# Loading the first two pairs' queries and keys four tokens to a partition, and transposing them on TensorE

## The chip, the cores and the metric

The kernel runs on one core of one Trainium2 chip. The metric is device time in microseconds (us) of one launch, the median of several runs. A profiled execution gives a trace beside it: the time of every instruction on TensorE (PE, with its weight loads as PEld), VectorE (DVE), ScalarE (ACT), GpSimd (POOL) and SyncE (SP), and of the transfers.

## The reference, cut to what matters

Attention with normalised queries and keys is followed by a gated feed-forward block.

```python
# q, k, v: (8, 12, 448, 64) float32; moe_w_*: float64, 768x1536, 768x1536, 1536x768
def rmsnorm(x, g):
    rms = np.sqrt(np.mean(x * x, axis=-1, keepdims=True) + 1e-06)
    return x / rms * g
q_n, k_n = (rmsnorm(q, g_q), rmsnorm(k, g_k))
scores = (1 / np.sqrt(64)) * np.matmul(q_n, k_n.transpose(0, 1, 3, 2))
attn = softmax(scores)                       # over the keys
x = np.matmul(attn, v) -> (8 * 448, 12 * 64) # token rows, heads side by side
g = x @ w_gate
out = (g / (1 + exp(-g)) * (x @ w_val)) @ w_out
```

## The kernel before, in words

The work is cut into 48 pairs: a pair is one batch and two heads, whose 2 x 64 head dimensions fill the 128 partitions. Two batches make a block of the feed-forward part; there are four blocks. The first 12 pairs ("early") come before any feed-forward work. The up products of a block (L1328, weights gate and value) and its down products (L1502) then fill TensorE, and the later pairs are worked in between the down products. The weights come as 64-bit floats. They are cast and summed into 15 combinations each (`convert`, L1120), written to DRAM (L1227) and read back as product weights (L1288). Six of the 24 weight pieces are converted among the early pairs, the others during the first block; those go into places that the early pairs use, after the last early pair has read them.

A pair is made by `attention` (L703). Its steps are these.

- `load` (L723): queries and keys, four loads each, one for each quarter of the partitions. A quarter holds one head and one half of the head dimension, so a row that is moved is 32 floats (128 bytes). All are issued by SP, but pair 0's keys by ACT.
- `square` (L754) on ACT, `summed` (L768) on DVE over each row of 32. Since a token's 64 values lie in two quarters, `swap` (L778, four ACT copies) exchanges the half sums and `both` (L782, DVE) adds them.
- `inverse_root` (L672): a logarithm and an exponential on ACT (L678, L679), three DVE steps (L684 to L686).
- `scale` (L795): two POOL multiplications, keys first.
- `transpose` (L811): two DVE transposes of 32x32 blocks. The queries go back into the buffer they were loaded in, and `queries` (L814, ACT) multiplies them by the gains' product `gg` (L1607) into the tile QT. The keys go to KT.
- `scores` (L840, PE), `exps` (L855, ACT), in four steps: keys 0 to 383 in three, the last 64 keys in a half step. Then `weighted` (L916, PE, values), `total` (L947, PE, sums of the exponentials), a reciprocal (L982, DVE), its spreading (L990, PE) and copy, addition and multiplication (L1005 ACT, L1008 and L1012 DVE). Sums of the finished pairs (L1049, L1053) feed the up products.

The loaded tiles have four buffers, so two pairs' queries and keys (`qk=4`, L547): the third pair's load waits until the first one's last reader is done. The tiles `t`, QT, KT, the two-bank score tile `st` and the output tile `at` have two each.

The order of the work is written by a planner, `Order` (L361). Every step is a piece with an engine, an assumed cost, a due time, the pieces it waits for and the buffers it takes. The planner runs a clock of its own through all the pieces and appends the instructions to each engine in the order that it finds. So a cost or a due time changes no instruction, only the order on each engine; on the chip each engine works through its queue in order. Early pairs are due from `LEAD`, one every `PAIR`, and everything later counts from these:

```python
LEAD, PAIR = 14.0, 9.0
FIRST = LEAD + EARLY * PAIR + 6.0
```

Of the kernel before, what the change touches and what calls it, by code (L numbers as in the profile page):

```python
# [477 lines left out]
def fast(  # L478
# [41 lines left out]
    nc = tc.nc  # L520
    B, H, S, D = q.shape
    DM = H * D
    DFF = moe_w_gate.shape[1]
    P = 128
    NJ = 4
# [5 lines left out]
    TB = 512  # L531
    NB = B // 2
    C = 32
# [2 lines left out]


    EARLY = 2 * NPAIR

    const = ctx.enter_context(tc.tile_pool(name="const", bufs=1))  # L540
    sbuf = ctx.enter_context(tc.tile_pool(name="sbuf", bufs=1))
# [5 lines left out]
        qk=4, v=2, t=2, QT=2, KT=2, e=4, ea=7, eh=2, sums=1, inv=1, rd=1, rows=3, st=2, at=2, ss=2,  # L547
        rr=4, ws=2, **{x + str(i): 1 for x in "vw" for i in range(6)},
# [6 lines left out]
    tiles = {}  # L555
# [10 lines left out]
    def take(name, key, shape):  # L566
        if name in ("e", "ea"):
            at = order.turn[name] % BUFS[name]
            tiles[name, key] = es[:, at] if at < BUFS["e"] else more_es[:, at - BUFS["e"]]
            return tiles[name, key]  # L570
        if name in OFTEN:
            at = OFTEN[name] + order.turn[name] % BUFS[name]
            tiles[name, key] = spare[:, ts(at, S)]
            return tiles[name, key]
        if name == "eh":
            at = order.turn["eh"] % BUFS["eh"]
            tiles[name, key] = more[:, at].rearrange("p (h q) -> p h q", h=2)
            return tiles[name, key]
        if name in WORK:
            at, size = WORK[name]  # L580
            at += order.turn[name] % BUFS[name] * size
            n = 1
            for length in shape[1:]:
                n *= length
            x = work[0 : shape[0], at : at + n]
            letters = "abcd"[: len(shape) - 1]
            x = x.rearrange(
                f"p ({' '.join(letters)}) -> p {' '.join(letters)}",
                **dict(zip(letters, shape[1:])),
            )  # L590
# [35 lines left out]
    many = const.tile([P, C], F32, name="many")  # L626
    halves = const.tile([P, 2, C], F32, name="halves")
    chosen = const.tile([P, 2, P], F32, name="chosen")
    gq2 = const.tile([P, 1], F32, name="gq2")
    gk2 = const.tile([P, 1], F32, name="gk2")  # L630
    gg = const.tile([P, 1], F32, name="gg")
# [1 line left out]

    LEAD, PAIR = 14.0, 9.0
    FIRST = LEAD + EARLY * PAIR + 6.0
    PRODUCT = 1.504
    UP, DOWN, BOTH = 30 * NG * PRODUCT, 90.7, 170.0
# [32 lines left out]
    def inverse_root(m, sums, of, when, rank=0.0):  # L672


        def estimate():
            ss = of()
            rr = take("rr", m, list(ss.shape))
            nc.scalar.activation(rr, ss, AF.Ln, scale=GAIN**-2)  # L678
# [24 lines left out]
    def attention(m):  # L703
# [14 lines left out]
        def add(*what, **more):  # L718
            return order.add(*what, rank=rank, **more)
# [2 lines left out]

        def load(x, src):  # L723
            def emit():
                to = take("qk", (m, x), [P, NC, C])
                for g in range(P // C):
                    rows = src[b, 2 * c + g // 2][:, ts(g % 2, C)]
                    queue.dma_start(to[ts(g, C)], rows.rearrange("(c i) f -> i c f", i=C))  # L728


            both = m == 0 and src is k
            queue = nc.scalar if both else nc.sync
            return add(
                "ACT" if both else "SP", 1.4 if both else 2.4, ready - 28.0, emit, takes=[("qk", (m, x))], kb=224, early=25.0,
                after=[staged.get(PAIRS)],
            )

        loaded = [load(x, src) for x, src in enumerate((q, k))]

        def load_values():  # L740
# [9 lines left out]

        def square(x):
            if x == 0:
                take("t", m, [P, 2, NC, C])
            nc.scalar.activation(tiles["t", m][:, x], tiles["qk", (m, x)], AF.Square)  # L754

        squares = []
        for x in range(2):
# [7 lines left out]


        def summed():
            nc.vector.tensor_reduce(  # L768
                out=take("ss", m, [P, 2, 2 * NC])[:, 0],
                in_=tiles["t", m].rearrange("p x c f -> p (x c) f"),  # L770
                axis=AX.X,
                op=ALU.add,
            )
# [12 lines left out]
        sums = add(  # L786
            "DVE", 1.1, ready - 17.0, summed, after=squares, uses=[("t", m)], takes=[("ss", m)]
        )
        sums = add("ACT", 0.9, ready - 16.0, swap, after=[sums], uses=[("ss", m)])
        sums = add("DVE", 0.15, ready - 15.0, both, after=[sums], uses=[("ss", m)])  # L790
        rr = inverse_root(m, sums, lambda: tiles["ss", m][:, 0], ready - 14.0, rank)

        def scale(x):
            rr = tiles["rr", m][:, ts(x, NC)].rearrange("p (c one) -> p c one", one=1)
            nc.gpsimd.tensor_tensor(  # L795
                out=tiles["t", m][:, x], in0=tiles["qk", (m, x)], in1=rr.to_broadcast([P, NC, C]),
                op=ALU.mult,
            )
# [7 lines left out]
        ]  # L806


        def transpose(x):
            to = take("KT", m, [P, S]) if x else tiles["qk", (m, 0)].rearrange("p c i -> p (c i)")  # L810
            nc.vector.transpose(to, tiles["t", m][:, x].rearrange("p c f -> p (c f)"))  # L811

        def queries():
# [2 lines left out]
                scale=gg,  # L816
            )

        kt = add(
            "DVE", 0.62, ready - 6.0, lambda: transpose(1), after=scaled[:1], takes=[("KT", m)],  # L820
            uses=[("t", m)],
        )
        qt = add(
            "DVE", 0.62, ready - 6.0, lambda: transpose(0), after=scaled[1:],
            uses=[("t", m), ("qk", (m, 0))],
        )
        qt = add(
            "ACT", 0.65, ready - 5.0, queries, after=[qt, gains], uses=[("qk", (m, 0))],
            takes=[("QT", m)],
        )  # L830
# [766 lines left out]
    for t, x in ((gq2, g_q), (gk2, g_k)):  # L1597
        col = x.rearrange("(d one) -> d one", one=1)
        nc.gpsimd.dma_start(t[0:64, :], col)
        nc.gpsimd.dma_start(t[64:128, :], col)  # L1600
    nc.vector.memset(chosen, 0.0)
    for i in range(P // C):
        h, half = divmod(i, 2)
# [94 lines left out]
```

## Time and profile before

| | |
|---|---|
| median of 3 runs | 1487.12 us |
| the runs | 1483.69 to 1489.3 us |
| profiled execution, first to last instruction | 1484.0 us (no further time of its own is given) |
| first product on PE | 14.66 us |
| first up product | 140.13 us |
| PE busy | 1425.0 us, 96% |
| DVE busy | 916.0 us, 62% |
| ACT busy | 681.5 us, 46% |
| POOL busy | 414.1 us, 28% |
| SP's first load of values issued | 7.50 us |

How to read it: a line of a timeline gives the start, the busy time, the engine, the line of the code, the operation with output and inputs, and in brackets how long the engine was idle before and who released it. "SPq" and "ACTq" are the queues where transfers are issued; the data lands later. A group of instructions has its busy time and the mean in ns of one. A product of 32-bit floats appears as two records. A line of stages gives, for each engine, its busy time and in brackets its instructions.

### The profile page before, as it was taken

The page shows a single profiled execution, that of the slowest core. Times are in us where ns is not written, and L with a number is a line of the kernel's source. Part 1 is how long each engine was busy: PE and PEld are TensorE (multiplying, and loading weights), DVE is VectorE, ACT ScalarE, POOL GpSimd, SP SyncE. Part 2 cuts the span into 40 slices and gives each one's busy share as a digit, 9 for nine tenths or more (in the row PEclk, how much of TensorE's full clock was granted, in tenths as well). Part 3 has the DMA queues.
Part 4 walks back from the last instruction along what each step waited for, and adds up shares of the span by engine and source line. Part 5 has one row for each costly group of instructions (what it writes and reads, how often), then busy time and mean ns, then how long its engine had stood idle before and what let it go on. Part 6 is the DMA issues. An engine that isn't in the chain of part 4 may idle for free.

```text
span 1484.0 us, 19470 instructions
## 1 busy us (share of the span) xinstructions
PE 1425.0 (96%) x6672; PEld 675.4 (46%) x6672; DVE 916.0 (62%) x1405; ACT 681.5 (46%) x1366; POOL 414.1 (28%) x468
## 2 busy tenths in 40 slices
PE   5789999999999999999999999999999999999998
PEld 2334544443444455544444445554444445555553
DVE  4777887877978544355886733454786854432533
ACT  6774544437775322445767422354676532122100
POOL 2454586636444100012544200011343410000000
PEclk9999999999999999999999999999999999999999
DMA  7767999974453432533344432352353442222235
GB/s 165 158 144 236 292 308 341 296 219 90 99 115 85 113 106 71 138 103 90 74 111 110 100 117 73 106 136 77 96 119 85 90 119 89 80 98 73 83 98 107
DMA packets 415921, 193.30 MB, mean 130 GB/s; under 512 B 324164, under 2 KB 397892, under 8 KB 409668
## 3 DMA queue, kind: packets, MB, share of 16 engines
q1 hardware_dynamic: 402688, 190.35, 48.0%
q10 hardware_dynamic: 12996, 1.61, 0.7%
q8 instruction: 55, 0.90, 0.3%
q14 instruction: 54, 0.44, 0.1%
q0 software_dynamic: 128, 0.00, 0.0%
HBM read 157.29 MB, written 34.60 MB: 129 GB/s over the span
## 4 chain that ended last, share of the span: by engine, by line
PE 73%; DVE 3%; ACT 2%; issue 1%; DMA 1%; SPq 1%; ACTq 0%; DVEq 0%
PE mm L1502 22%; PE mm L1328 20%; PE at L1328 20%; PE st L840 6%; PE at L916 5%; PE st L947 1%; ACT spare L1000 1%; ACT es L855 1%; DVE rd L982 1%; DMA out_dram<-spare 0%; SPq L728 0%; DVE ss L782 0%; DMA work<-in_k_dram 0%; DVE ss L768 0%; DVE sums L866 0%
## 5 line engine op out<-in xcount | busy, mean ns | idle before, releaser
L1328 PE MATMUL mm<-xs,ws 128*128 128x448 f32 x960 | 401.2, 540 | 4.4 <-DVE spare L1276 2.2
L1328 PE MATMUL at<-xs,ws 128*128 128x448 f32 x960 | 400.6, 540 | 4.1 <-DVE v L1274 2.6
L1328 PEld LDWEIGHTS mm<-xs,ws 128*128 128x128 f32 x960 | 181.5, 190 | 185.8 <-issue 173.8
L1328 PEld LDWEIGHTS at<-xs,ws 128*128 128x128 f32 x960 | 181.9, 190 | 184.6 <-issue 172.6
L795 POOL TENSOR_TENSOR work<-work,rr 128x448 f32<-128x448 f32 x96 | 105.9, 1122 | 503.5 <-DVE rr L686 245.2
L840 PE MATMUL st<-work 64*64 64x448 f32 (+1 forms) x1536 | 155.1, 508 | 27.3 <-ACT work L814 21.2
L1502 PE MATMUL mm<-gt,ws 128*128 128x448 f32 x448 | 177.2, 545 | 0.0
L1272 DVE TENSOR_TENSOR gt<-gt,mm 128x448 f32<-128x448 f32 x64 | 39.7, 621 | 185.1 <-PE mm L1328 171.3
L1502 PE MATMUL mm<-hs,ws 128*128 128x448 f32 x384 | 152.1, 545 | 0.9 <-DVE ss L684 0.9
L855 ACT ACTIVATE es<-st 128x896 f32<-128x896 f32 x129 | 114.3, 913 | 56.1 <-PE at L916 42.8
L860 POOL TENSOR_TENSOR sums<-es 128x896 f32<-128x896 f32 x36 | 75.7, 2104 | 195.8 <-PE st L947 83.2
L1402 ACT ACTIVATE st<-gt 128x448 f32<-128x448 f32 x96 | 52.4, 547 | 163.8 <-DVE gt L1276 85.9
L1000 ACT COPY spare<-rd 32x224 f32<-32x224 f32 x288 | 108.1, 375 | 35.0 <-DVE rd L982 30.7
L1502 PEld LDWEIGHTS mm<-gt,ws 128*128 128x128 f32 x448 | 82.9, 190 | 84.2 <-issue 81.0
L916 PE MATMUL at<-es,v 64*64 64x448 f32 x1032 | 110.2, 545 | 7.2 <-ACT xs L1005 3.3
L1270 ACT COPY gt<-mm 128x448 f32<-128x448 f32 x80 | 42.5, 531 | 141.5 <-PE mm L1328 141.4
L1502 PEld LDWEIGHTS mm<-hs,ws 128*128 128x128 f32 x384 | 71.1, 190 | 72.9 <-issue 70.9
L840 PEld LDWEIGHTS st<-work 64*64 64x64 f32 x1536 | 50.9, 134 | 108.7 <-issue 38.1
L1270 ACT COPY v<-at 128x448 f32<-128x448 f32 x96 | 51.1, 532 | 83.2 <-PE at L1328 80.0
L860 POOL TENSOR_TENSOR sums<-sums,es 128x896 f32<-128x896 f32 x36 | 78.7, 2187 | 2.8
L811 DVE STREAM_TRANSPOSE work<-work 128x448 f32<-128x448 f32 x96 | 59.2, 627 | 25.2 <-POOL work L795 23.1
L916 PEld LDWEIGHTS at<-es,v 64*64 64x64 f32 x1032 | 39.7, 134 | 67.4 <-issue 57.4
(150 smaller groups left out, 1568.7 us busy)
## 6 DMA issues: line engine op xcount, KB each, us to landing
ws<-up_sides SPq DMA_DIRECT2D x32, 1024.0 KB, 4.9
ws<-down_sides SPq DMA_DIRECT2D x16, 1024.0 KB, 5.0
ws<-down_sides SPq DMA_DIRECT2D x28, 512.0 KB, 4.0
ws<-up_sides SPq DMA_DIRECT2D x16, 768.0 KB, 4.6
work<-in_q_dram SPq DMA_DIRECT2D x192, 56.0 KB, 2.4
work<-in_k_dram SPq DMA_DIRECT2D x188, 56.0 KB, 2.5
out_dram<-spare SPq DMA_DIRECT2D x168, 56.0 KB, 1.9
v<-in_v_dram SPq DMA_DIRECT2D x96, 96.0 KB, 2.5
```

The lines of the kernel that those rows point to most:

```text
L795: nc.gpsimd.tensor_tensor(out=tiles["t", m][:, x], in0=tiles["qk", (m, x)], in1=rr.to_broadcast([P, NC, C]), op=ALU.mult,)
L811: nc.vector.transpose(to, tiles["t", m][:, x].rearrange("p c f -> p (c f)"))
L840: nc.tensor.matmul(st[ds(D * x, D), h, 0:n], tiles["KT", m][rows, ds(P * j + D * of_keys, D)], tiles["QT", m][rows, ds(Q * of_queries, n)] ...
L855: nc.scalar.activation(e, tiles["st", (m, j)][:, :, 0 : S * width(j) // P], AF.Exp)
L860: nc.gpsimd.tensor_tensor(out=to, in0=tiles["e", (m, 0)] if j == 1 else to, in1=e, op=ALU.add)
L916: nc.tensor.matmul(tiles["at", (m, x)][ds(D * h, D), queries], tiles["v", m][rows, j, h], tiles["e", (m, j)][rows, h], start=j == 0, stop= ...
L1000: nc.scalar.copy(inv[ds(D * h + C * to, C), ts(x, Q)], tiles["rd", m][ds(D * h + C * x, C)])
L1270: nc.scalar.copy(to, ps)
L1272: nc.vector.tensor_tensor(out=to, in0=old, in1=ps, op=ALU.add)
L1328: nc.tensor.matmul(ps(), w[:, at, which, c], xs[:, SLOT[x], c], start=fresh and c == 0, stop=c == NC2 - 1, skip_group_check=True,)
L1402: nc.scalar.activation(take(*act, [P, 2, TB])[:, 0, 0:S], to, AF.Silu)
L1502: nc.tensor.matmul(banks[s][:, 0:S], w[:, at, s, g], where[x][:, g], start=fresh and g == 0, stop=g == NG - 1, skip_group_check=True,)
```

## The change

For pairs 0 and 1 (`NATURAL`), a partition holds four consecutive tokens: 112 partitions (`R = S // NJ`), two heads, 4 x 64 values of each, so a row that is moved is 1 KB and queries or keys are one load. A token's 64 values lie in one partition. The square and the sum run on 112 partitions and rows of 512; the sum is over 64, and a small DVE addition takes the place of `swap` and `both`. `scale` writes the products in the order token quarter, head, dimension. Then TensorE transposes each quarter (112 tokens by 128) against an identity into a score tile in PSUM, keys first (`turn`). A copy out of PSUM restores the order of the tokens (`drain`): keys on DVE, queries on ACT with the gain. The identity is made on POOL at the start, before its first multiplication. After pair 0's second square, TensorE is given four products of 512 columns on pair 0's keys, whose results nobody reads. `LEAD` becomes 10.0, so all due times of early pairs and of what follows are 4 earlier. The other 46 pairs are worked as before.

In the built program, the order of the instructions differs on every engine within the early pairs; after PE's first up products nearly all of it is the same. ACT's order at the start is now: squares of pair 0 and of pair 1's queries, pair 0's root, the square of pair 1's keys, pair 1's root, pair 0's queries, its two first exponentials, pair 1's queries, a weight cast, pair 2's squares, pair 0's second large exponential, pair 2's swap and root, pair 3's squares, pair 0's third. PE's is: four dummy products, 8 transposes, half step and first step of pair 0's scores, 8 transposes, then more scores. SP's register load of the flag `fits` (L1665) stands among pair 4's loads, where it stood behind the first product weights.

```diff
+    NATURAL = (0, 1)
+    R = S // NJ
+    ident = const.tile([P, P], F32, name="ident")
-    LEAD, PAIR = 14.0, 9.0
+    LEAD, PAIR = 10.0, 9.0
...
         def load(x, src):
             def emit():
+                if natural:
+                    to = take("qk", (m, x), [R, 2, NJ * D])
+                    rows = src[b][2 * c : 2 * c + 2].rearrange("h (p j) d -> p h (j d)", j=NJ)
+                    queue.dma_start(to, rows)
+                    return
...
+            nc.scalar.activation(tiles["t", m][:, x], of, AF.Square)
+            if m == 0 and x:
+                for _ in range(4):
+                    nc.tensor.matmul(banks[0], chosen[0:R, 0], of, start=True, stop=True)
...
         def summed():
+            if natural:
+                ss = take("ss", m, [P, 2, 2 * NC])
+                sums = ss[0:R, 0, 0 : 4 * NJ]
+                nc.vector.tensor_reduce(
+                    out=sums, in_=tiles["t", m].rearrange("p x (n d) -> p (x n) d", d=D), axis=AX.X,
+                    op=ALU.add,
+                )
+                nc.vector.tensor_scalar_add(sums, sums, D * 1e-6)
+                return
...
-        sums = add("ACT", 0.9, ready - 16.0, swap, after=[sums], uses=[("ss", m)])
-        sums = add("DVE", 0.15, ready - 15.0, both, after=[sums], uses=[("ss", m)])
+        if not natural:
+            sums = add("ACT", 0.9, ready - 16.0, swap, after=[sums], uses=[("ss", m)])
+            sums = add("DVE", 0.15, ready - 15.0, both, after=[sums], uses=[("ss", m)])
...
         def scale(x):
+            if natural:
+                split = dict(h=2, j=NJ, d=D)
+                rr = tiles["rr", m][:, ts(x, 2 * NJ)].rearrange("p (h j one) -> p h j one", h=2, one=1)
+                nc.gpsimd.tensor_tensor(
+                    out=tiles["t", m][:, x].rearrange("p (j h d) -> p h j d", **split),
+                    in0=tiles["qk", (m, x)].rearrange("p h (j d) -> p h j d", d=D),
+                    in1=rr.to_broadcast([R, 2, NJ, D]), op=ALU.mult,
+                )
+                return
...
+        def turn(x):
+            if x:
+                take("st", (m, "turned"), [P, 2, TB])
+            turned = tiles["st", (m, "turned")][:, x]
+            for j in range(NJ):
+                nc.tensor.transpose(turned[:, ts(j, R)], tiles["t", m][:, x, ts(j, P)], ident[0:R, 0:R])
+
+        def drain(x):
+            turned = tiles["st", (m, "turned")][:, x, 0:S].rearrange("p (j r) -> p r j", j=NJ)
+            to = take("KT" if x else "QT", m, [P, S]).rearrange("p (r j) -> p r j", j=NJ)
+            if x:
+                nc.vector.tensor_copy(out=to, in_=turned)
+            else:
+                nc.scalar.activation(to, turned, AF.Copy, scale=gg)
...
+    make_identity(nc, ident)
     nc.vector.memset(chosen, 0.0)
```

More of the change, by code (lines that the diff above doesn't have):

```diff
@@ L676, in estimate @@
             ss = of()
-            rr = take("rr", m, list(ss.shape))
+            rr = take("rr", m, [P, 2 * NC])[0 : ss.shape[0], 0 : ss.shape[1]]
+            tiles["rr", m] = rr
             nc.scalar.activation(rr, ss, AF.Ln, scale=GAIN**-2)
@@ L733, in load @@
             return add(
-                "ACT" if both else "SP", 1.4 if both else 2.4, ready - 28.0, emit, takes=[("qk", (m, x))], kb=224, early=25.0,
+                "ACT" if both else "SP", 0.5 if natural else 1.4 if both else 2.4, ready - 28.0, emit, takes=[("qk", (m, x))], kb=224, early=25.0,
                 after=[staged.get(PAIRS)],
             )
+        natural = m in NATURAL
         loaded = [load(x, src) for x, src in enumerate((q, k))]
@@ L752, in square @@
             if x == 0:
-                take("t", m, [P, 2, NC, C])
-            nc.scalar.activation(tiles["t", m][:, x], tiles["qk", (m, x)], AF.Square)
+                take("t", m, [R, 2, 2 * NJ * D] if natural else [P, 2, NC, C])
+            of = tiles["qk", (m, x)]
+            if natural:
+                of = of.rearrange("p h f -> p (h f)")
+            nc.scalar.activation(tiles["t", m][:, x], of, AF.Square)
+            if m == 0 and x:
+                for _ in range(4):
+                    nc.tensor.matmul(banks[0], chosen[0:R, 0], of, start=True, stop=True)
         squares = []
@@ L788, in attention, with sums_of @@
         )
-        sums = add("ACT", 0.9, ready - 16.0, swap, after=[sums], uses=[("ss", m)])
-        sums = add("DVE", 0.15, ready - 15.0, both, after=[sums], uses=[("ss", m)])
-        rr = inverse_root(m, sums, lambda: tiles["ss", m][:, 0], ready - 14.0, rank)
-        def scale(x):
+        if not natural:
+            sums = add("ACT", 0.9, ready - 16.0, swap, after=[sums], uses=[("ss", m)])
+            sums = add("DVE", 0.15, ready - 15.0, both, after=[sums], uses=[("ss", m)])
+        def sums_of():
+            return tiles["ss", m][0:R, 0, 0 : 4 * NJ] if natural else tiles["ss", m][:, 0]
+        rr = inverse_root(m, sums, sums_of, ready - 14.0, rank)
+        def scale(x):
+            if natural:
+                split = dict(h=2, j=NJ, d=D)
[6 more added lines that the diff above has]
+                return
             rr = tiles["rr", m][:, ts(x, NC)].rearrange("p (c one) -> p c one", one=1)
@@ L817, in queries @@
             )
-        kt = add(
+        kt = qt = None
+        if natural:
+            of_turned = ("st", (m, "turned"))
+            kt, qt = [
+                add(
+                    "PE", 0.8, ready - 6.0, lambda x=x: turn(x), after=[scaled[1 - x]],
+                    uses=[("t", m)] + [of_turned] * (1 - x), takes=[of_turned] * x, mode="full",
+                )
+                for x in (1, 0)
+            ]
+            kt = add(
+                "DVE", 0.64, ready - 5.0, lambda: drain(1), after=[kt], takes=[("KT", m)],
+                uses=[of_turned],
+            )
+            qt = add(
+                "ACT", 0.6, ready - 5.0, lambda: drain(0), after=[qt, gains], takes=[("QT", m)],
+                uses=[of_turned],
+            )
+        kt = kt or add(
             "DVE", 0.62, ready - 6.0, lambda: transpose(1), after=scaled[:1], takes=[("KT", m)],
@@ L822, in attention @@
         )
-        qt = add(
+        qt = qt if natural else add(
             "DVE", 0.62, ready - 6.0, lambda: transpose(0), after=scaled[1:],
@@ L826, in attention @@
         )
-        qt = add(
+        qt = qt if natural else add(
             "ACT", 0.65, ready - 5.0, queries, after=[qt, gains], uses=[("qk", (m, 0))],
```

## The prediction, made before the run

> **What bounds the kernel now.** I read the page's chain of waits and then the busy time by stage, to learn which stage can still give time.
>
> ```profile
> PE 73%; DVE 3%; ACT 2%; issue 1%; DMA 1%; SPq 1%; ACTq 0%; DVEq 0%
> ```
>
> The chain that ended last is TensorE (PE) work for three quarters of the span. The stages, with columns PE, weight load, DVE, ACT, POOL, clock, DMA share, GB/s:
>
> ```profile
> 0.00:20.00 20.00, 5.34 (x40) 1.98 (x40) 7.47 (x23) 9.18 (x22) 6.56 (x16) 1.00 0.76 146
> 20.00:140.00 120.00, 100.21 (x1164) 44.84 (x1157) 92.71 (x151) 83.61 (x160) 59.96 (x91) 0.99 0.71 172
> 140.00:330.00 190.00, 183.62 (x487) 91.61 (x486) 154.01 (x231) 83.19 (x113) 112.42 (x218) 1.00 0.95 293
> ```
>
> PE idles 14.7 us in the first stage, 19.8 in the twelve early pairs (20 to 140), 6.4 in the first block's up products, and hardly after. So what starts the pairs earlier can move the whole run, if the pairs pass it on. The timeline of the start shows the chain to the first product:
>
> ```profile
> 5.85 0.58 ACT L754 ACTIVATE work<-work 128x448 f32<-128x448 f32 x1 [2.96 <-DMA work<-in_k_dram]
> 7.15 0.58 ACT L754 ACTIVATE work<-work 128x448 f32<-128x448 f32 x1 [0.73 <-DMA work<-in_k_dram]
> ...
> 7.76 1.09 DVE L768 TENSOR_REDUCE ss<-work 128x28 f32<-128x896 f32 x1 [4.38 <-ACT work L754]
> ...
> 8.88 0.88 ACT L778 COPY ss<-ss 32x28 f32<-32x28 f32 x4 [1.15 <-DVE ss L768]
> ...
> 10.02 0.23 ACT L678 ACTIVATE rr<-ss 128x28 f32<-128x28 f32 x1 [0.25 <-DVE ss L782]
> ...
> 11.39 1.83 POOL L795 TENSOR_TENSOR work<-work,rr 128x448 f32<-128x448 f32 x2 [7.79 <-DMA v<-in_v_dram]
> ...
> 13.94 0.67 ACT L814 ACTIVATE work<-work,gg 128x448 f32<-128x448 f32 x1 [0.44 <-DVE work L811]
> ...
> 14.66 5.02 PE L840 MATMUL st<-work 64*64 64x224 f32 x32 [14.66 <-ACT work L814]
> ...
> 15.19 2.54 SPq L728 DMA_DIRECT2D work<-in_q_dram  x4
> ...
> 21.25 1.88 SPq L728 DMA_DIRECT2D work<-in_q_dram  x4
> ...
> 23.94 1.04 ACT L754 ACTIVATE work<-work 128x448 f32<-128x448 f32 x2
> ```
>
> The load, square, sum, half swap, root, scale, transpose and gain follow each other with nothing beside them, to 14.66. The two SPq lines show a second effect: pair 2's q load leaves just after pair 0's L814 ended (14.61), pair 3's just after pair 1's ended (20.57 + 0.66), since they take the buffers that L814 reads. Third, the first scores, by shape:
>
> ```profile
> L840 PE MATMUL st<-work 64*64 64x448 f32 x24 | 4.2, 864 | 0.0
> L840 PE MATMUL st<-work 64*64 64x224 f32 x8 | 1.0, 604 | 14.7 <-ACT work L814 14.7
> L916 PE MATMUL at<-es,v 64*64 64x448 f32 x8 | 0.9, 536 | 0.0
> ```
>
> The same width takes 864 ns among the first and 536 soon after: a slow start, though the page's granted clock reads 9 there.
>
> [...] No trace here shows a TensorE transpose. [...] the old loads are rows of 128 B, and 0 to 10 us moves 112 GB/s at a DMA share of 0.76, where 140 to 150 us moves 315 at 0.99. [...]
>
> **The change, part by part.**
>
> *Loads.* Sixteen loads (four of them on ACT) become four: rows of 1 KB. K of pair 0 still leaves ACT at 1.63. Loads at that line took 1.8 to 5.7 us to land, median 3.1; 224 KB in one piece beside three more I put at 3.4, so 5.0 instead of 7.15: -2.1 (bounds -3.7 and 0). SP reaches the values' loads at 2.3 instead of 7.50, -5.2.
>
> *Norm of pair 0.* Rows are 512 wide on 112 partitions: square 0.58 x 512/448 = 0.66 (+0.08), reduce 1.09 x 1024/896 = 1.25 (+0.16). The swap and its add go: 8.85 to 10.02 was 1.17, a small add takes about 0.3: -0.85. Roots stay (10.02 to 11.17). From there to the first score it was 3.49. Now: two scales 2 x 0.93 x 512/448 = 2.14 with 0.2 ahead, four transposes 0.8 (224 columns take 0.38 at L990, two passes; so 112 take 0.19), drain 0.67, hops 0.25: 4.06, +0.57. The gain gg now stands on DVE behind pair 1's root steps and pair 0's key drain: +0.4 (0 to 0.8). Sum: -2.1 + 0.08 + 0.16 - 0.85 + 0.57 + 0.4 = -1.7. Scores start at about 12.9.
>
> *Dummy products.* Four of 512 columns, two passes each. A 448-column pass takes 1.504/4 = 0.376 at L1328, so 0.43 here, 0.86 at half clock. [...] The query transposes can't start before 10.7, so they cost nothing; all slow they end at 11.9 and cost 1.2. If they work, the first 16 records take the 1.36 us that the later group (26.47) takes. The first large exp started 17.24 - 14.66 = 2.6 after the scores; now 1.4: -1.2. It starts at 14.3, -2.9 in all.
>
> *Identity.* A memset and a select of 128x128 on POOL at 3.6; not in the trace. The nearest row, a 128x128 add at L1202, takes 0.45 to 0.5 us. Between 0 and 3 us it is covered by POOL's wait to 11.39 (now about 8.4); beyond 4 it delays every scale. I take 0.
>
> *Buffers.* Natural pairs free their q buffer after the scale, about 10.7 and 14.0, not after L814. With SP ahead, pair 2's k lands near 18.5 (squares were at 23.94) and pair 3's near 23 (28.65): -5.4.
>
> *Queue order.* ACT's queue now has pair 0's second and third large exps behind a weight cast and the squares of pairs 2 and 3, and PE has pair 1's transposes ahead of pair 0's later scores. Walked with the rows' durations: second exp 19.0 (was 18.73), third ends 24.5 (was 20.62), pair 1's last ends 29.8 (was 30.46). So pair 0 gets later, pair 1 equals, and pairs 2 and 3 are prepared 5 us sooner. SP's register load moves from 128.2 to about 20: 0.75 + 0.19 plus gaps, up to 1.4 us ahead of pair 4's loads. SP has slack there, I take 0.
>
> *What passes on.* DVE is 77% busy from 20 to 140. Before 30 us it did 2.56 + 4.91 + 4.37 = 11.8 us of work. In the new order it can do the memsets (1.2) and checks (0.6), norm and drains of pairs 0 and 1 (2 x 2.8), norm and transposes of pairs 2 and 3 (2 x 2.9), the first join (0.6) and part of a reciprocal (1.0): 14.8, 3.0 ahead. The exps give 2.9, the loads 5.4; I take 3.2 for the end of the pairs. After that, nearly all queues stand in the old order. The next weights take the places that the last early pair leaves, so they move too: of PE's 6.4 idle us in that stage most wait for DVE, 0.87 for weights. I take full carry; the bounds are 0 and 3.2. The profiled execution has a span of 1484.0 and shows nothing around it; its own sum is 1480.8. The runs' median is 1487.12, 3.1 above, so: 1487.1 - 3.2 = 1483.9.
>
> **Rivals.**
>
> *Swallowed* (0.20): the pairs are held by DVE and by loads landing late (ACT stood 2.56 us for pair 5's keys at 54.98), or the first block waits longer for weights, its DMA share being 0.95. For it: pair 1's exps gain only 0.7. Against: DVE idled 6.7 us at 25 and 3.86 at 55. Result 1487.1.
>
> *Cold anyway* (0.12): the dummies end, PE idles[...]; or they end late. The 1.2 is lost, and up to 1.2 more hides the transposes: 3.2 - 1.7 = 1.5, so 1485.6.
>
> *All of it* (0.12): DVE fills its early holes and the loads' 5.4 comes through, with the reorder worth another 1: 1487.1 - 6.4 = 1480.7.
>
> *Slower by ACT's queue* (0.11): pair 0's third exp stands behind the squares of pair 3. If that pair's keys land behind a 1152 KB weight block (at 264 GB/s 4.4 us), at 27.5, pair 1's exps end at 34.3 and not 30.46: +3.9. The same order again at pairs 4 and 5 gives as much: +7.9, 1495.0. It decides from a landing at about 23.7. Against: DMA share was only 0.55 from 20 to 30.
>
> **How the numbers follow.** Forecast 0.45 at 1483.9. Half a per cent, 7.4 us, is about what a measurement of this kernel tells from no change; the three runs lie 5.6 apart. Faster by that needs under 1479.7: the most favourable part of "all of it" and of the forecast, 0.10. Slower needs over 1494.6: 0.10. The rest, 0.80, is within. The range of 1479.0 to 1490.5 holds the forecast, cold and swallowed cases with 3 us of spread and half of "all of it"; it leaves out the slower one.
>
> **What would show it.** First score near 12.9 and the first large exp near 14.3; 448-column scores near 540 ns from the start; dummies over by 10.5; pair 2's squares near 18.5 and pair 3's near 23; first up product at 137 and not 140.13; last first-block product 3 us before 328.4. It is wrong if ACT waits for pair 3's keys past 25, if a POOL select runs past 8 us, or if the first up product comes early and the block's weight waits grow by as much.

## The result, and the profile after

After the change the median is 1483.66 us (20 runs, 1481.1 to 1485.94), before it is 1487.33 (20 runs, 1483.69 to 1489.3). The ratio is 0.9977, 95% interval 0.9971 to 0.9983: about 3.4 us less. The profiled execution after spans 1482.6 us and its run took 1484.42. That difference of 1.8 lies around every profiled execution below, so the profiled one of before (1484.0) was a run of about 1485.8, 1.5 under its median, and that of after lies 0.8 over its own. Two single traces therefore differ by only 1.4 us, and no conclusion here rests on the two spans.

The chain of waits of the kernel after looks as before: TensorE for three quarters.

```profile
PE 73%; ACT 3%; DVE 3%; issue 1%; DMA 1%; SPq 1%; ACTq 0%; DVEq 0%
```

The stages of the kernel after, columns as in the prediction (PE, weight load, DVE, ACT, POOL, clock, DMA share, GB/s):

```profile
0.00:20.00 20.00, 11.06 (x39) 5.33 (x40) 6.59 (x20) 6.54 (x12) 7.46 (x18) 0.91 0.72 161
20.00:140.00 120.00, 105.47 (x1185) 46.74 (x1184) 91.39 (x152) 85.08 (x161) 54.46 (x81) 0.94 0.68 169
140.00:330.00 190.00, 184.28 (x490) 92.23 (x489) 156.59 (x234) 84.79 (x118) 118.93 (x228) 1.00 0.95 293
```

PE is busier in the first two stages (11.06 and 105.47, were 5.34 and 100.21), but 6.75 us of it are dummies, and in the second stage part of the busy time is products at half clock (0.94, was 0.99). So busy time alone shows no gain. The start has to be read step by step; the timeline of the kernel after:

```profile
1.61 0.41 ACTq L732 DMA_DIRECT2D work<-in_k_dram  x1
3.92 0.29 POOL masks.py:199 TENSOR_SCALAR_AFFINE_SELECT ident<-ident 128x128 f32<-128x128 f32 x1
6.71 1.15 ACT L767 ACTIVATE work<-work 112x512 f32<-112x512 f32 x2 [2.29 <-DMA work<-in_k_dram]
6.83 6.75 PE L770 MATMUL mm<-work,chosen 112*128 112x512 f32 x8 [6.83 <-DMA work<-in_k_dram]
7.38 1.22 DVE L787 TENSOR_REDUCE ss<-work 112x16 f32<-112x1024 f32 x1 [2.65 <-ACT work L767]
8.84 0.22 ACT L682 ACTIVATE rr<-ss 112x16 f32<-112x16 f32 x1 [0.97 <-DVE ss L791]
10.07 2.04 POOL L827 TENSOR_TENSOR work<-work,rr 112x512 f32<-112x512 f32 x2 [5.85 <-DVE rr L690]
13.41 0.93 PE L853 MATMUL st<-ident,work 112*128 112x112 f32 x8
14.38 0.62 DVE L859 COPY work<-st 128x448 f32<-128x448 f32 x1 [2.24 <-PE st L853]
15.51 0.16 DVE L1680 SCALAR_TENSOR_TENSOR gg<-gq,gk 128x1 f32<-128x1 f32 x1
15.77 0.63 ACT L861 ACTIVATE work<-st,gg 128x448 f32<-128x448 f32 x1 [3.13 <-DVE gg L1680]
16.45 1.02 PE L912 MATMUL st<-work 64*64 64x224 f32 x8 [2.11 <-ACT work L861]
```

The first score starts at 16.45, which is 1.8 later than before (14.66), though the run is faster. Four things are to be seen. The keys' landing lets the square start at 6.71. The dummies end at 13.58, and the key transposes wait for that: their scale was done near 11.1. The copies out of PSUM follow each other, and the second waits for `gg`, which DVE makes at 15.51 behind pair 1's root steps.

The first products of the kernel after by shape (mean ns is the number after the busy time):

```profile
L770 PE MATMUL mm<-work,chosen 112*128 112x512 f32 x8 | 6.7, 1025 | 6.8 <-DMA work<-in_k_dram 6.8
L912 PE MATMUL st<-work 64*64 64x224 f32 x8 | 1.0, 605 | 2.1 <-ACT work L861 2.1
```

The scores of 224 columns take 605 ns, as long as the 604 of before: the dummies did not make them faster. The next view, four short stretches of the kernel after (columns of the stages), shows why:

```profile
6.30:9.60 3.30, 2.77 (x4) 1.25 (x5) 1.63 (x4) 1.88 (x5) 0.00 (x0) 1.00 0.63 101
9.70:13.00 3.30, 3.30 (x6) 1.24 (x5) 2.37 (x4) 0.55 (x3) 2.04 (x2) 1.00 0.95 294
13.10:16.40 3.30, 1.24 (x10) 0.74 (x8) 1.21 (x5) 0.63 (x1) 0.76 (x1) 1.00 0.86 157
16.50:19.80 3.30, 3.30 (x21) 1.65 (x22) 0.00 (x0) 1.31 (x2) 1.18 (x2) 0.50 0.38 63
```

The clock column is the one ahead of the last two. It says 1.00 in the first two rows too, where the passes took 1025 ns (in e7 the median pass took 592): this trace's first record of the clock is at 13.03, and ahead of it the column says nothing. From 13.1 the 1.00 is real (eight transposes in 0.93 us), and it is 0.50 from 16.5, when the scores begin. Behind the dummies the clock was at 1.00, and by the time of the first score it was at 0.50.

### The profile page after: what moved, and what is told of

Same layout as the page of the kernel before. It is cut to its first block, busy times and chain, and to the rows that moved or that the text cites. A ratio compares the mean times of both kernels' runs of the same rounds, so it can differ in the third digit from the quotient of the medians.

```text
span 1482.6 us, 19482 instructions
## 1 busy us (share of the span) xinstructions
PE 1435.1 (97%) x6696; PEld 680.7 (46%) x6696; DVE 914.8 (62%) x1403; ACT 680.7 (46%) x1358; POOL 416.0 (28%) x470
## 4 chain that ended last, share of the span: by engine, by line
PE 73%; ACT 3%; DVE 3%; issue 1%; DMA 1%; SPq 1%; ACTq 0%; DVEq 0%
PE mm L1574 22%; PE mm L1400 20%; PE at L1400 20%; PE st L912 6%; PE at L988 5%; PE st L1019 1%; ACT spare L1072 1%; ACT es L927 1%; SPq L737 1%; DVE rd L1054 1%; DVE ss L807 0%; DMA work<-in_k_dram 0%; DMA out_dram<-spare 0%; DVE ss L793 0%; ACT ss L803 0%
## 5 line engine op out<-in xcount | busy, mean ns | idle before, releaser
L834 POOL TENSOR_TENSOR work<-work,rr 128x448 f32<-128x448 f32 x92 | 101.8, 1126 | 480.1 <-DVE rr L690 353.3
```

The source lines that it names most:

```text
L834: nc.gpsimd.tensor_tensor(out=tiles["t", m][:, x], in0=tiles["qk", (m, x)], in1=rr.to_broadcast([P, NC, C]), op=ALU.mult,)
```

## The experiments

The theory after the first reading: the start became no earlier, so the gain must come from the order of the instructions, which the prediction had put at nothing. The rival: it comes from the new data path (fewer loads, no swaps, SP free sooner). Two times of each trace are compared, the first score and the first up product, with the stage between them:

| kernel | first score, us | first up product, us | stage, us | median, us | ratio to before, 95% interval |
|---|---|---|---|---|---|
| before | 14.66 | 140.13 | 125.5 | 1487.33 | |
| after | 16.45 | 139.92 | 123.5 | 1483.66 | 0.9977, 0.9971 to 0.9983 |
| e4, before again | 14.60 | 139.06 | 124.5 | 1486.41 | 0.9999, 0.9990 to 1.0007 |
| e2, due times only | 14.54 | 140.97 | 126.4 | 1486.45 | 0.9999, 0.9990 to 1.0007 |
| e9, weights behind keys | 14.68 | 141.53 | 126.9 | 1487.59 | 1.0000, 0.9991 to 1.0008 |
| e6, new path, old order | 16.66 | 143.71 | 127.1 | 1486.20 | 0.9994, 0.9987 to 1.0000 |
| e5, old path, new order | 16.57 | 137.90 | 121.3 | 1483.14 | 0.9970, 0.9959 to 0.9981 |
| e11, as e5, gain first | 16.23 | 136.93 | 120.7 | 1484.14 | 0.9978, 0.9971 to 0.9985 |
| e1, no dummies | 16.22 | 136.62 | 120.4 | 1483.21 | 0.9976, 0.9966 to 0.9987 |
| e3, early dummies | 16.62 | 140.20 | 123.6 | 1484.30 | 0.9979, 0.9971 to 0.9988 |
| e7, twelve dummies | 23.30 | 144.99 | 121.7 | 1490.37 | 1.0018, 1.0008 to 1.0028 |
| e10, start mended | 13.08 | 136.33 | 123.3 | 1479.91 | 0.9955, 0.9942 to 0.9969 |
| e8, all early natural | 16.51 | 135.62 | 119.1 | 1492.60 | 1.0034, 1.0023 to 1.0046 |
| e12, preparation first | 16.34 | 147.1 | 130.8 | 1494.03 | 1.0047, 1.0032 to 1.0061 |

Each ratio is to runs of before that were made beside that kernel, so it is not the quotient of two medians of the table. The times of the first score, the first up product and the stage are those of one trace each.

### Taking the parts away: e1, e2, e3, e4

e1 is the kernel after without the dummies:

```diff
-            if m == 0 and x:
-                for _ in range(4):
-                    nc.tensor.matmul(banks[0], chosen[0:R, 0], of, start=True, stop=True)
```

> The changed kernel without its four dummy products; the order on every engine is otherwise the same. In the profile of the changed kernel the dummies ran at half clock from 6.83 to 13.58 and the key transposes started at 13.41, while the scaled keys were there at about 11.1. Theory A (the dummies are a cost where they stand): first score at about 15 and not 16.45, and the run is equal to the changed kernel or up to 1.5 us faster, 0.9967 to 0.9977 of before. Rival (the dummies pay by warming the array): the first scores become slower still, and the run loses 1 to 2 us, 0.9985 to 0.999 of before.

Measured: 0.9976 beside 0.9977 with them, as the theory had it; but the first score came at 16.22, not at about 15. Its start, PE and the chain ahead of it:

```profile
9.77 0.22 ACT L682 ACTIVATE rr<-ss 112x16 f32<-112x16 f32 x1 [0.97 <-DVE ss L788]
12.10 2.01 PE L850 MATMUL st<-ident,work 112*128 112x112 f32 x8 [12.10 <-POOL work L824]
15.53 0.64 ACT L858 ACTIVATE work<-st,gg 128x448 f32<-128x448 f32 x1 [1.96 <-DVE gg L1677]
16.22 2.52 PE L909 MATMUL st<-work 64*64 64x224 f32 x16 [2.11 <-ACT work L858]
```

In this trace pair 0's keys landed 0.9 later than in after (7.62 and 6.69), so the root began at 9.77 and not 8.84. From the root to the first score it is 6.45 us, with dummies 7.61: the dummies cost 1.2 us at this place. The eight transposes take 2.01 here and 0.93 behind the dummies. A difference of 1.2 at the start doesn't show in the medians (1483.21 and 1483.66, intervals overlap).

e2 is the kernel before with the new due times only; it tells the change of order that they bring alone from that which the new pieces bring. e4 is the kernel before, unchanged.

```diff
-    LEAD, PAIR = 14.0, 9.0
+    LEAD, PAIR = 10.0, 9.0
```

> The kernel before with LEAD 10 in place of 14 and nothing else: the order on PE and POOL stays word for word, 26 lines of DVE, 42 of ACT and 20 of SP change. Theory A (the gain comes from the pairs' new data path and the order that follows from it): within 1 us of before, 0.9993 to 1.0007. Rival (the gain is the shifted due times): as the changed kernel, 0.997 to 0.998.

> The kernel before, unchanged: a second trace, and what the comparison makes of no change. 1.000 within 0.0006. If stages vary from one execution to the next, the first up product (140.13 in the first profile) and the span (1484.0) move by 1 to 4 us and show in which stage; if the first profile is typical they stay within 0.5 us.

Both measured 0.9999, so the due times alone are worth nothing, and the comparison itself is good to about 0.1%. In e2, PE's and POOL's queues are those of before; 26 instructions of DVE, 42 of ACT and 20 of SP stand elsewhere. But all of these stand behind the first up product (on SP near 265 us, on DVE from about 610). Among the early pairs e2 runs in the order of before, so it says that the due times change nothing there without the new pieces; it is no test of the new order. In e4 the first up product came 1.1 us earlier than in the first trace of the same kernel, so a stage varies by that much at least.

e3 has eight dummies of 256 columns on a constant tile, without waiting for a load, in place of the four:

```diff
-            if m == 0 and x:
-                for _ in range(4):
-                    nc.tensor.matmul(banks[0], chosen[0:R, 0], of, start=True, stop=True)
...
+    for _ in range(8):
+        nc.tensor.matmul(
+            banks[0][:, 0 : 2 * P], chosen[:, 0], chosen.rearrange("p x f -> p (x f)"),
+            start=True, stop=True,
+        )
```

> The changed kernel with its dummy products replaced by eight of 256 columns on the constant tile, which need no load; they should run from about 2 to 9 us. Theory A (dummies late, in the way of the transposes): first score at 14 to 15, and if the array stays at full clock until then the first 448-column scores take near 540 ns and not 951; 1 to 2 us faster than the changed kernel, 0.9965 to 0.997. Rival (the start is not on the path that sets the end): the start moves and the run stays at 0.9977 within 0.0006.

Measured 0.9979, and the first score came at 16.62, not at 14 to 15. The dummies start at 1.86 and end at 7.15, PE then idles 5.34 us, and the transposes at 12.49 take 2.01 us again, as in e1, at a clock of 0.50: dummies that early brought the transposes nothing.

### Order or data path: e5, e6, e11

In these kernels the planner is replaced by a fixed list of pieces, so that one kernel's instructions are issued in the other's order:

```diff
-    def run(self, lookahead=400):
...
+    def run(self):
+        left, at = [], 0
+        for step in STEPS.split():
+            at += int(step)
+            left.append(self.pieces[at])
+        while left:
+            i = next(i for i, piece in enumerate(left) if self.start(piece) is not None)
+            piece = left.pop(i)
```

e5 has the loads and transposes of before in the order of after; apart from the replaced instructions its queues are those of after. e6 has the loads, transposes and dummies of after in the order of before.

> The kernel before (old loads, swap, DVE transposes, no dummies) with the pieces of work emitted in the changed kernel's order; swap stands behind the sum and the old transposes and gain stand where the new drains stand. Theory B (the gain is the new order of the early pairs' work on the engines, which the new pieces gave to the planner): 0.997 to 0.9985 of before. Rival theory C (the gain is the new data path: larger rows, earlier free buffers): 1.000 or slower, up to 1.003, since the order was made for shorter steps.

> The changed kernel's data path for pairs 0 and 1, dummies included, with the pieces of work emitted in the order of the kernel before. Theory B (order): 0.9995 to 1.001 of before, although pair 2's and 3's loads go earlier. Theory C (data path): 0.997 to 0.9985. If the two effects add, this ratio times that of the old path in the new order gives the 0.9977 of the changed kernel.

Measured: e5 0.9970, the whole gain without any of the new instructions; e6 0.9994, at most a small part of it with all of them. That settles order against path. Whether the two add isn't told: the product of the two ratios is 0.9964, against 0.9977 for after, and each is good to about 0.001. The stage from the first score to the first up product says it again: in the order of before it took 124.5 to 127.1 us (five traces, mean 126.0), in that of after 120.4 to 123.6 (after, e1, e3, e5, e7, e10, e11; mean 122.1). From the first up product to the end both orders take the same, 1344.3 and 1344.2 us. So the order is worth 3.9 us of this stage; one trace of an order can lie 3 us from another. The 3.9 is idle time of PE: between these two marks it idles 17.1 to 19.8 us in the five traces of the old order (mean 18.2) and 12.3 to 16.0 in the seven of the new (mean 14.3).

What it does, in stretches of the kernel before:

```profile
20.00:30.00 10.00, 8.01 (x100) 3.56 (x92) 4.37 (x8) 8.72 (x18) 0.47 (x1) 1.00 0.55 96
40.00:50.00 10.00, 7.90 (x100) 3.37 (x98) 8.27 (x17) 7.33 (x15) 3.34 (x5) 1.00 0.73 180
50.00:60.00 10.00, 6.38 (x85) 2.58 (x81) 5.67 (x11) 6.46 (x14) 3.96 (x9) 1.00 0.63 155
```

and of e5, which has the same instructions:

```profile
20.00:30.00 10.00, 3.63 (x32) 1.21 (x32) 4.19 (x9) 8.16 (x21) 1.84 (x2) 0.81 0.83 186
40.00:50.00 10.00, 9.30 (x112) 3.83 (x108) 9.23 (x17) 9.00 (x17) 4.34 (x7) 1.00 0.53 95
50.00:60.00 10.00, 10.00 (x120) 4.45 (x116) 8.30 (x15) 9.16 (x17) 7.78 (x14) 1.00 0.90 268
```

The new order loses at first: PE is busy 3.6 of 10 us instead of 8, since ACT prepares pairs 2 and 3 between pair 0's exponentials, and ACT's copy of pair 0's output starts at 35.59 (before 24.93). From 30 to 70 PE then idles 0.7 us in all, where that of before idles 8.5, of which 2.1 at 40 to 50 and 3.6 at 50 to 60. The other traces say the same: 6.2 to 9.6 us in the five of the old order, 0.4 to 3.8 in the seven of the new. By the same copy, pair 4 is ahead in the new order (72.44, was 73.55), pair 5 once more behind (82.24, was 80.68), and from pair 7 on each is 1.5 to 2.9 ahead, pair 11 at 135.49 (was 137.72).

e11 is e5 with `gg` made right behind pair 0's root, one step of the list moved:

```diff
-    '1 1 32 1 -32 1 1 31 -30 1 1 29 -28 1 28 359 -358 1 1 -30 31 -30 55 -54 30 -43 14 1 29 24 -52 29 -27 '
+    '1 1 32 1 -32 1 1 31 -30 1 1 29 -28 1 -10 38 359 -358 1 1 -30 31 -30 55 -54 30 -29 1 29 24 -52 29 -27 '
```

> The old data path in the new order (0.997 of before) with the gain moved right behind pair 0's root on DVE. First score at 14.6, as before, and not 16.57. If the start is passed on: 0.9955 to 0.996. Rival (lost again): 0.9965 to 0.9975.

Measured 0.9978, a little above the rival's range, its interval overlapping that of e5. The first score came at 16.23, not at the expected 14.6: in the old path the queries' gain doesn't wait for `gg`, because the DVE transposes come later still.

### Is a late start passed on: e7 and e10

e7 runs twelve dummies instead of four.

```diff
-                for _ in range(4):
+                for _ in range(12):
```

> The changed kernel with twelve dummy products in place of four, so that the first transposes and pair 0's scores come some 7 to 13 us later (half clock until about 13.6 us, 0.84 us a pass, then either clock). Theory: the start of the scores has slack, because pair 0's later exponentials wait in ACT's queue behind the squares of pairs 2 and 3 anyway; then the run loses less than half of the delay of the first score, 0.9977 to 1.000. Rival (the recorded view: the start is passed on): the run loses the whole delay, 1.002 to 1.006.

The first score came 6.85 us later than after's, the median 6.7 us (6.1 by the ratios). So the delay is passed on, and the theory of slack has fallen. PE then is fast: 16 scores of 224 columns in 1.36 us (after 2.52), the first large exponential 1.43 behind the first score (after 2.59), which doesn't pay for the delay.

e10 mends the start of the kernel after: no dummies, pair 0's keys on SP right behind its queries, and `gg` on DVE right behind pair 0's root (a step of the list); all else in after's order.

```diff
-            both = m == 0 and src is k
+            both = False
...
-            if m == 0 and x:
-                for _ in range(4):
-                    nc.tensor.matmul(banks[0], chosen[0:R, 0], of, start=True, stop=True)
```

> The changed kernel's data path and order without dummies, with two moves: pair 0's keys are loaded on SP right after its queries (they landed 5 us after issue, behind pair 1's), and the gain stands on DVE right behind pair 0's root. First score at 12 to 13.5 and not 16.2. If the start is passed on, as twelve dummies' 6.85 us was, the run is 3 to 4 us faster than the changed kernel: 0.9945 to 0.996. Rival (a gain at the start is lost to the waits for loads): 0.9965 to 0.998.

Measured 1479.91 (5 runs), 0.9955, the fastest of all: 3.75 us under after by the medians, 3.3 by the ratios, for a first score 3.4 earlier. Its start:

```profile
4.82 0.63 ACT L873 ACTIVATE work<-work 112x512 f32<-112x512 f32 x1 [0.21 <-DMA work<-in_k_dram]
7.38 0.20 ACT L788 ACTIVATE rr<-ss 112x16 f32<-112x16 f32 x1
9.68 2.01 PE L956 MATMUL st<-ident,work 112*128 112x112 f32 x8 [9.68 <-POOL work L930]
11.73 0.63 DVE L962 COPY work<-st 128x448 f32<-128x448 f32 x1 [1.07 <-PE st L956]
12.39 0.63 ACT L964 ACTIVATE work<-st,gg 128x448 f32<-128x448 f32 x1 [1.23 <-DVE work L962]
13.08 2.52 PE L1015 MATMUL st<-work 64*64 64x224 f32 x16 [1.38 <-ACT work L964]
```

The keys' square starts at 4.82 (6.71), and the queries' gain no longer waits for `gg` but for the key copy. Beside e1, which differs by the two moves alone, the root begins 2.4 us earlier (7.38, was 9.77) through the keys, and the first score 3.1 earlier; the rest is `gg`'s. The median is 3.3 us under that of e1, where the two intervals overlap a little. The traced run is the slowest of e10's five (1482.43), so that its stage of 123.3 is likely long. So the new path can give an earlier start, about what the prediction said, once pair 0's keys stand second among the loads and the gain isn't late. e7 and e10 both say that a microsecond at the start is nearly a microsecond at the end. Not tried: the loads and transposes of before in the new order with pair 0's keys second on SP. How much of e10's start belongs to the new path, and how much to the place of the keys, is therefore open.

### Where in the order: e9, e12, e8

e9 is the kernel before with one thing moved: SP's fourth load of a weight piece stands behind pair 5's queries and keys. In before, ACT waited 2.56 us for those keys. The order of SP's queue, the only one that differs (the register load of `fits` comes forward too, to about where after has it):

```diff
+TensorLoad fits
+DMACopy work<-in_q_dram 32x14x32 x4
+DMACopy work<-in_k_dram 32x14x32 x4
 DMACopy gt<-in_moe_w_val_dram 128x2x128 x2
 DMACopy gt<-in_moe_w_val_dram 128x3x128
 DMACopy gt<-in_moe_w_val_dram 128x128 x2
-DMACopy work<-in_q_dram 32x14x32 x4
-DMACopy work<-in_k_dram 32x14x32 x4
...
-TensorLoad fits
```

> The kernel before with one thing changed: on SP the load of the fourth weight piece stands behind pair 5's queries and keys, as in the changed kernel's order, and not ahead of them (SP's register load moves too). All other engines keep the old order. Theory D (the new order gains because pair 5's keys no longer land behind a weight piece: before, ACT waited for them 2.56 us and DVE stood 3.86 us at 55): pair 5's squares at about 50 and not 54.98, and 0.997 to 0.9985 of before. Rival (the gain is the order of the work on ACT, DVE and PE, more pairs prepared ahead of the exponentials): 0.9993 to 1.0007.

Measured 1.0000. Two stretches of e9:

```profile
50.00:60.00 10.00, 8.78 (x112) 3.71 (x105) 8.36 (x17) 8.89 (x17) 7.29 (x13) 1.00 0.89 252
60.00:70.00 10.00, 6.63 (x52) 2.36 (x56) 6.12 (x7) 6.06 (x9) 4.60 (x7) 0.91 0.65 126
```

The hole at 50 to 60 is filled (PE 8.78, was 6.38), and the next stretch has it instead (6.63, was 9.28), with ACT waiting 3.87 us for the next queries. In this trace the hole is moved, not closed. But its place isn't fixed: in e4, the unchanged kernel, ACT waited only 0.48 us for pair 5's keys and PE was busy 8.96 us at 50 to 60, with the hole at 40 to 50 (7.23). So the wait of 2.56 belongs to that one execution, and it is the ratio that says the theory has fallen.

e12 is the kernel before with only the preparation of pairs in the order of after (a list again); PE's queue is that of before to the instruction. DVE's order around pair 0's reciprocal, for one:

```diff
 TensorReduce ss<-work 128x28
-TensorTensor xs<-xs,at 128x448
-Reciprocal rd<-mm 128x224
 TensorScalarPtr ss<-ss 128x28
...
 TensorReduce ss<-work 128x28
+TensorTensor xs<-xs,at 128x448
+Reciprocal rd<-mm 128x224
 StreamTranspose work<-work 128x448 x2
```

> The kernel before, with its own loads, transposes and instructions; only the pieces that prepare a pair (loads of queries and keys, squares, sums, swaps, roots, scales, DVE transposes, gains) stand at the places that they have in the order of the kernel after, and all else, scores and exponentials and weights too, keeps the order of before. TensorE's queue is then that of before, instruction for instruction. Theory one, the order of after gains because the preparation of the pairs runs further ahead of the exponentials: ratio 0.997 to 0.9985, and from the first score to the first up product about 122 to 123.5 us. Theory two, the gain needs TensorE's and the exponentials' order too (pair 1's first products ahead of pair 0's later ones): ratio 0.9993 to 1.0010, and 125 to 127 us for that stage. The first score is expected at 14.6 to 16.6 us in both.

Measured 1.0047: neither theory's number, and the theory that preparation ahead is the gain by itself has fallen. DVE and PE of e12 around 30:

```profile
29.11 1.09 DVE L873 TENSOR_REDUCE ss<-work 128x28 f32<-128x896 f32 x1 [1.80 <-ACT work L859]
30.64 1.55 DVE L1087 RECIPROCAL rd<-mm 128x224 f32<-128x224 f32 x1
32.24 1.23 PE L1095 MATMUL mm<-rd,chosen 128*128 128x224 f32 x4 [4.15 <-DVE rd L1087]
```

Pair 0's reciprocal stands on DVE behind pair 3's sum, and that behind the square of keys that landed near 28.5. It starts at 30.64 (before 26.61), and PE, whose old order has the spreading product ahead of pair 1's work, stands still for 4.15 us. This is kin to the prediction's slower rival: the cause is the same, keys of pair 3 that land late, but what waits for them is DVE's reciprocal and not ACT's exponential. That the price comes near the rival's 1495.0 is in part chance. The first score of e12 is 1.7 later too, and after the wait PE is at half clock for some 6.8 us (the mean of 30 to 40 is 0.66); over 20 to 140 the mean clock is 0.91 (before 0.99). In the kernel after, PE has pair 1's products at that place.

e8 brings all twelve early pairs in the new way, and the planner orders them:

```diff
-    NATURAL = (0, 1)
+    NATURAL = tuple(range(2 * NPAIR))
```

> The changed kernel with all twelve early pairs loaded four tokens to a partition and transposed on TensorE. Theory C (the data path helps every pair it is used for: rows of 1 KB, no swap, 0.9 us of ACT less a pair): 0.993 to 0.9965. Theory B (it is the order): anything between 0.995 and 1.004, the planner making another order. Against it: 16 transposes and a score tile more for each pair on TensorE.

Its first up product is the earliest of all (135.62), and yet it is slower than before, 1.0034: theory C has fallen. PE of e8 in the first block:

```profile
180.87 1.67 PE L1400 MATMUL at<-xs,ws 128*128 128x448 f32 x4
190.47 3.32 PE L1400 MATMUL mm<-xs,ws 128*128 128x448 f32 x4 [7.93 <-DVE st L1246]
```

and SP of e8:

```profile
172.52 6.05 SPq L1208 DMA_DIRECT2D work<-in_moe_w_gate_dram  x3
178.61 0.96 SPq L1210 DMA_DIRECT2D work<-in_moe_w_gate_dram  x2
180.06 0.52 SPq L1299 DMA_DIRECT2D up_sides<-gt  x1
180.68 3.72 SPq L1360 DMA_DIRECT2D ws<-up_sides  x2
```

The releaser named is a DVE step that ended at the same moment and has nothing to do with `ws`. The product reads product weights whose two loads leave SP at 180.68 and 183.26. By the trace's semaphores the first of them landed at 190.33, 9.7 us after it was issued, and the product began at 190.47. PE is idle for 7.93 us, and the clock is at half from 186.3 to 196.5 (the mean of 180 to 230 is 0.90); some 6 us of PE's work fall there, about 3 us more than at full clock (an estimate, half of the 6). Together that is the 11 us by which e8 takes longer from the first up product to the end (1355.2, both orders above 1344.2). In the kernel after, the same two loads leave within 0.80 us, from 179.95 on, and have landed by 187.2, and PE goes on without a wait. Here the prediction's rival "swallowed" is seen: a gain in the pairs is lost in the first block. Not tried: e8 with the weight loads earlier on SP.

## Why the prediction was right or wrong

The number was right (1483.9 for 1483.66, and the sign), the working was not: two terms failed and about cancelled, which is luck. Of the signs that the prediction named for itself nearly none came: the first score was to be near 12.9 and came at 16.45, the first large exponential near 14.3 and came at 19.04, the dummies were to be over by 10.5 and ended at 13.58, the early 448-column scores were to take 540 ns and took 951, the first up product was to come at 137 and came at 139.92.

*Start: the first large exponential was to be 2.9 earlier, and was 1.8 later (17.24 to 19.04); the first score was to be 1.7 earlier, and was 1.8 later.* By its own steps:

- *Loads, -2.1: failed.* Landing was read at the square's start. 7.15 became 6.71, -0.4, and this trace was the best of six: in e1, e3, e6, e7 and e8, with the same first loads, pair 0's keys landed between 7.3 and 8.0. The estimate took the median of landings at that line; but these keys are third in the order of issue, behind pair 0's and pair 1's queries. In e10, where they are second, they are squared at 4.82. The prediction also took the low rate of the first 10 us (112 GB/s) as a sign of short rows, which no trace of before showed by itself; with rows of 1 KB these 10 us moved 151 GB/s, still about half of the later 315, so short rows are at most part of it.
- *Square, sum, no swap, -0.61: right.* From landing to root 1.70 + 1.17 became 1.89 + 0.24, -0.74.
- *Root to score, +0.57 and +0.4 for the gain: failed.* It went from 4.64 to 7.61, +3.0. From the end of the root's steps (9.92): key scale 1.02 with 0.15 ahead, 2.32 of standing behind the dummies, transposes 0.93, key copy 0.62, wait for pair 1's root steps and `gg` 0.77, query copy 0.63, hops 0.09; sum 6.53. The working had let the dummies end before the transposes, had one copy where two follow each other, and put 0.4 where 0.77 came. It counted two scales (2.14) where one stands on the path, and 0.8 for four transposes where eight took 0.93; these two errors went the other way.
- *Dummies: the branch "all slow" came, for the first passes at least.* They began at 6.83, not 5.0, ran 6.75 us, and ended at 13.58. That half of the passes would run at full clock was the author's estimate, which no trace of before showed. The cost of 1.2 that the prediction gave for this case is what e1 shows. The worth of scores at full clock was sized right (first large exponential 1.4 behind the first score in e7 and e8, 2.6 in after), but in after the clock was at 0.50 by the first score.
- *Identity, 0: right.* Memset and select took 0.21 and 0.29 us, done at 4.2, under POOL's wait.
- *Buffers, -5.4: the landing was right, the squares were not.* Pair 2's keys landed at 17.4 (18.5 predicted) and pair 3's at 23.1 (23). But their squares stood in ACT's queue behind other work until 22.71 (23.94 before) and 26.51 (28.65): the prediction had taken landing and square for one. Nor is the landing what the gain needs: in e5 pair 2's keys landed only at 22.7.

*Queue order: no gain of its own predicted, -3.9 measured (e5, e6).* The step "pair 0 gets later, pair 1 equals" walked the queues only to pair 1; measured, pair 0's third large exponential ended at 28.4 (24.5 walked), pair 1's last at 35.2 (29.8), both later. The gain comes after that, from 30 on, where the walk had stopped. The ledger of DVE (+3.0 before 30 us) also failed: it did 11.3 us of work there, not 14.8 (before: 11.8).

*What passes on: right in kind.* e7 and e10 carry a shifted start to the end, and from the first up product to the end both orders take the same time. e8 shows a limit.

The two measured terms give 1.8 - 3.9 = -2.1 from single traces; the medians give -3.4 to -3.7. The rest is within the 3 us by which traces of one order differ.

*Rivals.* "Cold anyway" was right about the first scores (they ran at a clock of 0.50) and wasn't what set the time. "Slower by ACT's queue" didn't come in after: pair 3's keys landed at 23.1, and both its squares ran at 26.51 without waiting for a load. e12 shows what such a wait costs where keys land at 28.4.

What stays open is which pieces of the new order give the 3.9 us. The due times alone don't (e2, whose early pairs run in the old order), one moved load doesn't (e9), the preparation alone costs (e12: +4.8 on the stage). That PE's and the exponentials' order is needed with the preparation's is what is left, and no run shows it by itself.

## What to carry to other kernels

When a change passes through a planner, first replay the old instructions in the new order and the new instructions in the old: here that gave the whole gain to the order, and the new data path was worth nothing until its start was mended. Walk a new order further than the first pair that it touches; here it lost 11 us on the first, and was 2 us ahead at the twelfth. The dummy products made the first scores faster only where the clock was still at 1.00 when these began (e7 and e8: 16 scores in 1.36 us; after and e3: 2.52). A value that everything waits for (here pair 0's keys, and the gain `gg`) belongs at the head of its queue.

## What the runs showed of the hardware

*The dummies' worth hung on the clock at the first score.* The stretches of after above show it, and e8 has the same four dummies 0.9 us later:

```profile
8.80:12.10 3.30, 3.30 (x5) 1.27 (x4) 2.63 (x7) 0.95 (x3) 1.11 (x2) 1.00 0.51 143
12.20:15.50 3.30, 2.20 (x12) 1.22 (x10) 1.86 (x5) 0.43 (x2) 0.83 (x1) 1.00 0.96 293
15.60:18.90 3.30, 2.32 (x24) 1.29 (x24) 0.15 (x2) 2.10 (x3) 2.04 (x2) 1.00 1.00 273
```

In after, the stretch in which the dummies ended held 1.24 us of PE's work in 3.3, and the next was at a clock of 0.50; in e8 it held 2.20, the clock stayed at 1.00, and its first 16 scores took 1.36 us and not 2.52. How much work it takes to keep the clock at 1.00, these two don't show. The dummies themselves began slow: in after their eight passes started 0.85 us apart (the first two 0.98), and the first transpose 0.48 behind the last pass.

*The transposes, too, took about twice as long at half clock.* Eight took 0.93 us in after, at a clock of 1.00; in e3 they took 2.01 at 0.50, and 1.75 in this stretch:

```profile
18.70:22.00 3.30, 3.30 (x20) 1.71 (x16) 0.63 (x1) 1.40 (x2) 0.00 (x0) 0.50 0.65 106
19.06 1.75 PE L850 MATMUL st<-ident,work 112*128 112x112 f32 x8
```

Of the scores behind them, from 20.75 on, the first eight records took 1.65 us and sixteen 2.44, so the second eight added 0.79. Whether the transposes had a part in that, no run shows.

*A short wait cost twice.* In after, PE idled 3.21 us at 25 to 28, and its next 16 records of 448 columns took 3.27 us at a clock of 0.50, where before such 16 took 1.73 behind a wait of 0.85. Ahead of the first score, 2.11 us of idle time were followed by a clock of 0.50 in after; the same 2.11 in e7 and e8 were followed by 16 scores in 1.36 us. So in these traces the length of the wait alone doesn't tell what follows.

*The first two loads landed sooner than the later ones, by whichever queue.* Pair 0's and pair 1's queries and keys are four loads of 224 KB each. In after the first two landed 3.0 and 3.3 us after their issue, both on SP; the third, pair 0's keys, took 5.1 on ACT's queue, and the fourth 5.4 on SP's. In e10, all on SP, the squares that waited for the first two began 3.2 and 3.6 after their issue, and that for the third 5.1. In e1, e3, e6, e7 and e8 the square of the third began 5.7 to 6.4 after its issue on ACT. So in these traces the late landing goes with the place in the order and not with the queue: pair 0's keys were squared at 6.71 as third and at 4.82 as second. Why the later ones take longer, no run shows.
